# Adding a zero row to the last, 64-row tile of a K dimension of 448, and zero columns to its transposes, with earlier staging of Q and K and later Pool constants

## The chip, the cores and the metric

The kernel runs on one NeuronCore of a Trainium2 chip. Its metric is the device time of one execution in microseconds (us), as the median of several executions. A profile is the hardware's own record of one execution; its span is a little shorter than the time (204.2 us against 205.9 us for the same execution of the kernel before).

Engines are named as the profile names them: PE is TensorE (matmuls), PEld its weight loads, DVE is VectorE, ACT is ScalarE, POOL is GpSimd, SP issues most of the DMAs.

"Clock" is the share of PE's full clock that the chip granted. This kernel has windows of 3.41 us in which PE gets half of it.

## The reference

One transformer block on x of 2048 tokens by 448 (bf16): LayerNorm with conditioning, dilated local attention (16 heads of 28, window 8, step 2), LayerNorm again, an MLP of 448 to 1792 to 448, and two gated residuals.

```python
mod = (_silu(c) @ w_mod).reshape(c.shape[0], 6, 1, -1)
sa, ca, ga, sb, cb, gb = ...                      # six rows of 448
h = _layernorm(x) * (1 + ca) + sa
x = x + ga * _A_ref(h, A_wqkv, A_wo)              # qkv = h @ wqkv; attention; @ wo
h = _layernorm(x) * (1 + cb) + sb
x = x + gb * _B_ref(h, B_w1, B_b1, B_w2, B_b2)    # layernorm, gelu(y @ w1 + b1) @ w2 + b2
```

What matters is that D = 448 = 3 * 128 + 64. Every product that sums over D takes three tiles of 128 rows and one of 64.

## The kernel before

All work is added to a small planner as tasks with an engine, an assumed duration, and reads and writes. The planner runs a list schedule with these durations and emits the instructions in that order.

```python
S, D, H, DH, F = 2048, 448, 16, 28, 1792
KT, KR = 4, 64
KW = (128, 128, 128, KR)          # rows of each K tile
...
    # QK projection, for 2 or 4 token blocks (n = 256 or 512 columns), 8 groups
    for kt in range(KT):
        nc.tensor.matmul(pq.t[:], lhsT=wqk_m(kt, m), rhs=hT[0:KW[kt], kt, c0:c0 + n],
                         start=(kt == 0), stop=(kt == KT - 1))
...
    # V projection, once for each of 17 attention blocks
    for kt in range(KT):
        nc.tensor.matmul(pv.t[:], lhsT=hT[0:KW[kt], kt, k0:k0 + BK], rhs=Wv[0:KW[kt], kt, :],
                         start=(kt == 0), stop=(kt == KT - 1))
...
    # transposes of LN1's output; kt = 3 is 64 columns wide
    nc.tensor.transpose(out=ptr.t[0:KW[kt], k, bi * 128:(bi + 1) * 128],
                        in_=zbufs[b % NZ][:, kt * 128:kt * 128 + KW[kt]], identity=ident[:])
...
    # MLP: here the last tile has 65 rows already, since row 64 carries the bias
    kp = KW[kt] + (kt == KT - 1)
    nc.tensor.matmul(p1.t[:, f, :], lhsT=w1_s[0:kp, kt, (fq + f) * 128:(fq + f + 1) * 128],
                     rhs=yT.t[0:kp, kt, :], start=(kt == 0), stop=(kt == KT - 1))
```

The weights of Q and K are staged side by side in one tile and spread by head into `Wqk` (heads of 28 padded to 32); Q's spread is on DVE, most of K's on ACT. The conditioning columns (`ps_col`) are 32 matmuls of one column each, 8 of them with 64 rows. Attention itself uses small tiles on purpose: 28-row logits (`lt`) and 32-column sums (`pd`, `po`), four side by side in the array.

The softmax here doesn't subtract the row's maximum and nothing guards it: scores larger than these inputs give would overflow.

Of the kernel before, what the change touches and what calls it, by code (L numbers as in the profile page):

```python
# [9 lines left out]
BF16 = mybir.dt.bfloat16  # L10
ACT = mybir.ActivationFunctionType
# [3 lines left out]
DP = 512  # L15
KT, KR = 4, 64
KW = (128, 128, 128, KR)
HP = 32
FT = F // 128
WIN = 8  # L20
# [7 lines left out]
EPS = 1e-5  # L28
DEN_SCALE = 2.0 ** -32
EXP_SET = "natural_log_exp_and_others"  # L30
QKE = "ADAADAAD"
SPREAD = (("DVE", "DVE"), ("ACT", "DVE"))
PHASES = [
    (range(0, 5), [0]),
    (range(5, 9), [1, 2]),
# [164 lines left out]
def kernel(  # L200
# [35 lines left out]
    def sb(room, shape, dtype, name):  # L236
        return Buf(room, lambda: wk.tile(shape, dtype, name=name, tag=room, bufs=ROOM[room]), name)
# [36 lines left out]
    rs_all = cst.tile([128, 3, NBLK], FP32, name="rs_all")  # L274
    NX1P = 8
    NZ, NY, NV = 4, 4, 3
    zbufs = [cst.tile([128, D], BF16, name=f"zbuf{i}") for i in range(NZ)]
    ybufs = [cst.tile([128, DP], BF16, name=f"ybuf{i}") for i in range(NY)]
    vbufs = [cst.tile([128, H, HP], BF16, name=f"vbuf{i}") for i in range(NV)]
    x1p_ring = cst.tile([128, NX1P, D], FP32, name="x1p_ring")  # L280
    wm_st = sb("hm", [128, KT, 2 * D + KR], BF16, "wm_st")
    wqk_st = sb("hm", [128, KT, 2 * D + HP - DH], BF16, "wqk_st")
    wmod2 = [sb("hm", [128, KT, 2 * D], BF16, f"wmod2{i}") for i in range(2)]

    def tok_col(b):
# [27 lines left out]
    def load_x(b0, b1):  # L313
        load(lambda: nc.sync.dma_start(out=x_all[:, b0:b1, :], in_=xv[b0 // 8, :, b0 % 8:(b1 - 1) % 8 + 1, :]),
             (b1 - b0) * 128 * D * 2, [f"x{b}" for b in range(b0, b1)])
# [2 lines left out]
    add("DVE", 0.1, lambda: nc.vector.memset(one1[:], 1.0), writes=["one1"], rank_add=500)  # L318
    add("DVE", 0.1, lambda: nc.vector.memset(c_row[:, D:DP], 0.0), writes=["c_tail"], rank_add=500)
    add("ACT", 0.4, lambda: nc.scalar.dma_start(out=c_row[:, 0:D], in_=c), writes=["c_row"], late=2.0, rank_add=500)  # L320
    tbl0 = add("ACT", 1.28, lambda: nc.scalar.preload_act_table_set(EXP_SET), rank_add=400)
    load_x(0, 2)
    load_k(lambda: wm_st.t[:], w_mod[:, 0:2 * D + KR], "wm", [wm_st])
    load_k(lambda: wqk_st.t[:, :, 0:D + HP - DH], A_wqkv[:, 0:D + HP - DH], "wq", [wqk_st])
    load_k(lambda: wqk_st.t[:, :, D + HP - DH:], A_wqkv[:, D + HP - DH:2 * D + HP - DH], "wk", [wqk_st])
    load_x(2, 4)
    load_k(lambda: Wv[:], A_wqkv[:, 2 * D:3 * D], "wv")
    load_x(4, 8)
    for i in range(2):
        load_k(lambda i=i: wmod2[i].t[:], w_mod[:, (2 + 2 * i) * D:(4 + 2 * i) * D], f"wmod2{i}", [wmod2[i]])  # L330
    add("DVE", 0.3, lambda: nc.vector.memset(wo_s[:], 0.0), writes=["wo"], rank_add=400)
    wo_v = A_wo.rearrange("(ft r d) n -> r d ft n", r=4, d=DH)
    for r in range(4):
# [12 lines left out]
                F * D, [f"w2l{i}"])  # L346


    def pool(us, fn, writes, reads=(), rank_add=300):
        add("POOL", us, fn, writes=writes, reads=reads, rank_add=rank_add)  # L350

    pool(0.1, lambda: nc.gpsimd.memset(eps_col[:], EPS), ["eps"])
    pool(0.2, lambda: nc.gpsimd.memset(ident[:], 0.0), ["ident"])
    pool(0.3, lambda: nc.gpsimd.affine_select(out=ident[:], in_=ident[:], pattern=[[-1, 128]],
                                              compare_op=ALU.not_equal, fill=1.0, base=0, channel_multiplier=1),
         ["ident"])
    def one_row():
        nc.gpsimd.memset(one_cb[:], 0.0)
        nc.gpsimd.memset(one_cb[2 * HP:3 * HP, :], 1.0)
# [88 lines left out]
    def mod_cols():  # L448
        for v in range(2):
            for j in range(KT):  # L450
                for kt in range(KT):
                    nc.tensor.matmul(pscol.t[:, v * KT + j:v * KT + j + 1],  # L452
                                     lhsT=wm_st.t[0:KW[kt], kt, v * D + j * 128:v * D + (j + 1) * 128],
                                     rhs=silu_bf[0:KW[kt], kt:kt + 1], start=(kt == 0), stop=(kt == KT - 1))

    P.wrote(add("PE", 2.0, mod_cols, reads=["silu", "wma", "wmb"], bufs=[pscol, wm_st]), pscol)
    add("DVE", 0.08, lambda: nc.vector.tensor_copy(out=mod_col[:, 0:KT], in_=pscol.t[:, 0:KT]), bufs=[pscol],
        writes=["sa"])
    add("DVE", 0.08, lambda: nc.vector.tensor_scalar_add(out=mod_col[:, KT:2 * KT], in0=pscol.t[:, KT:2 * KT], scalar1=1.0),
# [18 lines left out]
    def front_ln(bs, on_act):  # L478
        for b in bs:
            stats(lambda b=b: x_all[:, b, :], [f"x{b}"], b, mv1, b)  # L480
        if on_act:
            rstd_act(mv1, 0, bs[0], len(bs))
        else:
            rstd_pool(mv1, 0, bs[0], len(bs))
        for b in bs:
            normalize(lambda b=b: zbufs[b % NZ][:], lambda b=b: x_all[:, b, :], mv1, 0, b, [f"x{b}"], [f"z{b % NZ}"])
        n = len(bs)
        c0 = tok_col(bs[0])
        for half, eng in enumerate(("DVE", "ACT")):
            ptr = ps_one([128, 2, 128 * n], "ptr", BF16)  # L490

            def tr(half=half, ptr=ptr):
                for bi, b in enumerate(bs):
                    for k in range(2):
                        kt = 2 * half + k
                        nc.tensor.transpose(out=ptr.t[0:KW[kt], k, bi * 128:(bi + 1) * 128],  # L496
                                            in_=zbufs[b % NZ][:, kt * 128:kt * 128 + KW[kt]],
                                            identity=ident[:])

            P.wrote(add("PE", 0.13 * n, tr, reads=["ident"] + [f"z{b % NZ}" for b in bs], bufs=[ptr]), ptr)  # L500
            for k in range(2):
                evac_h(2 * half + k, ptr, k, c0, 128 * n, eng, bs)

    def spread(half, k0, k1, eng):

        kw = KW[k0]
        key = "wq" if half == 0 else "wk"
        o = Wqk[0:kw, k0:k1, half]

        def i():  # L510
            a = wqk_st.t[0:kw, k0:k1, half * D:(half + 1) * D]
            return bass.AP(a.tensor, a.offset, [a.ap[0], a.ap[1], [DH, H], [1, HP]])

        reads = [h + ("a" if k0 < KT - 1 else "b") for h in ("wq", "wk")[0:half + 1]]
        if eng == "DVE":
            add("DVE", 0.08 + 0.134 * (k1 - k0), lambda: nc.vector.tensor_copy(out=o, in_=i()), reads=reads, bufs=[wqk_st], writes=[f"W{half}{k0}"])
        else:
            add("ACT", 0.17 + 0.366 * (k1 - k0), lambda: nc.scalar.copy(out=o, in_=i()), reads=reads, bufs=[wqk_st], writes=[f"W{half}{k0}"])

    def wqk_m(kt, m):  # L520
        return Wqk[0:KW[kt], kt, m // 4, m % 4 * 4:m % 4 * 4 + 4, :].rearrange("p r e -> p (r e)")

    def front_qk(bs, engs):
        n, c0 = 128 * len(bs), tok_col(bs[0])
        for m in range(8):
            pq = ps_one([128, n], "pq")

            def mm(m=m, pq=pq):
                for kt in range(KT):
                    nc.tensor.matmul(pq.t[:], lhsT=wqk_m(kt, m), rhs=hT[0:KW[kt], kt, c0:c0 + n],  # L530
                                     start=(kt == 0), stop=(kt == KT - 1))

            P.wrote(add("PE", 4 * n / 2400 + 0.02, mm,
                        reads=[f"W{m // 4}0", f"W{m // 4}{KT - 1}"]
                        + [f"h{kt}_{b}" for kt in range(KT) for b in bs], bufs=[pq]), pq)
            dst = (qT if m < 4 else kT)[:, m % 4, c0:c0 + n]
            w = [f"{'q' if m < 4 else 'k'}{m % 4}_{b}" for b in bs]
            if engs[m] == "D":
                add("DVE", 0.07 + n / 960, lambda dst=dst, pq=pq: nc.vector.tensor_copy(out=dst, in_=pq.t[:]), bufs=[pq],
                    writes=w)  # L540
            else:
                add("ACT", 0.13 + n / 1400, lambda dst=dst, pq=pq: nc.scalar.copy(out=dst, in_=pq.t[:]), bufs=[pq], writes=w)  # L542


    def mods():
        pb = ps_one([128, D], "pb")

        def mm():
            for kt in range(KT):
                for i in range(4):  # L550
                    nc.tensor.matmul(pb.t[HP * i:HP * i + HP], lhsT=silu_bc[0:KW[kt], kt, :],
                                     rhs=wmod2[i // 2].t[0:KW[kt], kt, i % 2 * D:(i % 2 + 1) * D],
                                     start=(kt == 0), stop=(kt == KT - 1), tile_position=(0, HP * i))

        P.wrote(add("PE", 1.1, mm, rank_add=150, reads=["silu_bc"] + [f"wmod2{i}{h}" for i in range(2) for h in "ab"],
                    bufs=[pb] + wmod2), pb)
        add("ACT", 0.6, lambda: nc.scalar.activation(out=mod_rows[:], in_=pb.t[:], func=ACT.Identity, bias=one_cb[:]),
            bufs=[pb], reads=["one_cb"], writes=["mod_rows"])
# [23 lines left out]
    def attention(b, tbl, prev_w1):  # L582
# [5 lines left out]

        def vmm():
            for kt in range(KT):  # L590
                nc.tensor.matmul(pv.t[:], lhsT=hT[0:KW[kt], kt, k0:k0 + BK], rhs=Wv[0:KW[kt], kt, :],  # L591
                                 start=(kt == 0), stop=(kt == KT - 1))

        P.wrote(add("PE", 0.76, vmm, reads=["wva", "wvb"] + PADK + [f"h{kt}_{t}" for kt in range(KT) for t in tb], bufs=[pv, vbuf]), pv)
        P.wrote(add("ACT", 0.45, lambda: nc.scalar.copy(out=vbuf.t[:, :, 0:DH],  # L595
                                                        in_=pv.t[:].rearrange("p (h d) -> p h d", h=H)),
                    bufs=[pv, vbuf], reads=["vpad"]), vbuf)
# [237 lines left out]
```

## Time and profile before

| kernel before | |
|---|---|
| time, median of 3 | 205.52 us (205.34 to 206.44) |
| profiled span, mean clock | 204.2 us, 0.982 |
| PE / DVE / ACT busy | 95% / 65% / 58% |
| half-clock windows in the profile | at 9.1 and 36.4 us, and one at the very end |

The page of the kernel before: busy time, then busy tenths in 40 slices of 5.1 us each, then the granted clock in tenths.

```profile
PE 193.9 (95%) x1709; PEld 107.3 (53%) x1709; DVE 132.5 (65%) x342; ACT 117.7 (58%) x168; POOL 45.1 (22%) x88
...
PE   7699997899999999999999999999999989999992
...
DVE  5476478989999859689813699585179668502102
...
PEclk9879999699999999999999999999999999999999
```

Its chain that ended last, by engine:

```profile
PE 85%; DMA 6%; DVE 5%; ACT 2%; SPq 0%; issue 0%; DVEq 0%
```

So PE limits. But how a busy PE spends its time doesn't show in busy shares. It shows on the row of the weight loads. Groups of lines, shapes kept apart; columns are busy us, mean ns, then idle time just before these instructions and what ended it:

```profile
L720 PEld LDWEIGHTS <-w_s 65*128 65x128 bf16 x112 | 10.8, 96 | 1.4
...
L530 PEld LDWEIGHTS <-Wqk 128*128 128x128 bf16 x120 | 9.3, 98 | 10.0 <-issue 4.2
...
L530 PEld LDWEIGHTS <-Wqk 64*128 64x128 bf16 x40 | 3.7, 93 | 14.2 <-issue 14.2
...
L591 PEld LDWEIGHTS <-hT 64*128 64x128 bf16 x17 | 1.6, 93 | 6.3 <-issue 6.3
```

The 40 weight loads of 64 rows at L530 (QK) have 14.2 us of idle before them for which the profile names no releaser ("issue"). The 112 loads of 65 rows at L720 (W1) have none. The timeline of the weight loads shows it beat by beat (start, duration, instruction, idle before):

```profile
20.46 0.44 PEld L530 LDWEIGHTS <-Wqk 64*128 64x128 bf16 x4 [0.21 <-issue]
21.11 0.44 PEld L530 LDWEIGHTS <-Wqk 64*128 64x128 bf16 x4 [0.21 <-issue]
21.75 0.44 PEld L530 LDWEIGHTS <-Wqk 64*128 64x128 bf16 x4 [0.21 <-issue]
```

Each group of four begins 0.65 us after the last, where four matmuls of 256 columns at their own pitch (110 ns) need 0.44 us. The missing 0.21 us stands before the 64-row load.

The windows view shows the stretch where other engines are full too (columns: window, length, then busy us and instructions of PE, PEld, DVE, ACT and POOL, granted clock, DMA share, GB/s):

```profile
24.00:30.00 6.00, 6.00 (x70) 2.49 (x69) 3.02 (x6) 5.18 (x9) 0.00 (x0) 1.00 0.27 65
30.00:36.00 6.00, 4.23 (x87) 2.39 (x88) 5.35 (x11) 6.00 (x10) 0.00 (x0) 1.00 0.95 301
36.00:42.00 6.00, 5.48 (x35) 1.71 (x34) 5.30 (x16) 3.49 (x7) 1.02 (x1) 0.72 0.87 269
42.00:48.00 6.00, 6.00 (x25) 1.92 (x24) 5.78 (x16) 2.04 (x4) 2.55 (x3) 1.00 0.01 3
```

### The profile page before, as it was taken

The page shows a single profiled execution, that of the slowest core. Times are in us where ns is not written, and L with a number is a line of the kernel's source. Part 1 is how long each engine was busy: PE and PEld are TensorE (multiplying, and loading weights), DVE is VectorE, ACT ScalarE, POOL GpSimd, SP SyncE. Part 2 cuts the span into 40 slices and gives each one's busy share as a digit, 9 for nine tenths or more (in the row PEclk, how much of TensorE's full clock was granted, in tenths as well). Part 3 has the DMA queues.
Part 4 walks back from the last instruction along what each step waited for, and adds up shares of the span by engine and source line. Part 5 has one row for each costly group of instructions (what it writes and reads, how often), then busy time and mean ns, then how long its engine had stood idle before and what let it go on. Part 6 is the DMA issues. An engine that isn't in the chain of part 4 may idle for free.

```text
span 204.2 us, 4212 instructions
## 1 busy us (share of the span) xinstructions
PE 193.9 (95%) x1709; PEld 107.3 (53%) x1709; DVE 132.5 (65%) x342; ACT 117.7 (58%) x168; POOL 45.1 (22%) x88
## 2 busy tenths in 40 slices
PE   7699997899999999999999999999999989999992
PEld 2445443233457346635584437468644747666750
DVE  5476478989999859689813699585179668502102
ACT  2246399626937997466568983674858175431230
POOL 8200200119242203134300053162032306200000
PEclk9879999699999999999999999999999999999999
DMA  6999239900110200010140100401200211201011
GB/s 189 299 333 259 83 93 328 315 10 3 27 29 0 53 3 0 5 26 0 26 55 0 48 0 0 100 0 29 67 3 16 60 41 34 42 9 48 3 44 45
DMA packets 19000, 13.91 MB, mean 68 GB/s; under 512 B 9246, under 2 KB 18403, under 8 KB 18980
## 3 DMA queue, kind: packets, MB, share of 16 engines
q1 hardware_dynamic: 18978, 13.64, 24.9%
q8 instruction: 13, 0.21, 0.5%
q14 instruction: 7, 0.06, 0.1%
q10 hardware_dynamic: 2, 0.00, 0.0%
HBM read 9.70 MB, written 1.84 MB: 56 GB/s over the span
## 4 chain that ended last, share of the span: by engine, by line
PE 85%; DMA 6%; DVE 5%; ACT 2%; SPq 0%; issue 0%; DVEq 0%
PE p L720 24%; PE p L740 21%; PE pq L530 17%; PE pw L670 6%; PE pv L591 6%; PE ptr L496 3%; DMA wm_st<-in_w_mod_dram 3%; DMA mod_bc<-mod_hbm 2%; PE lt L604 2%; PE pd L631 2%; PE po L635 1%; PE pwm L395 1%; DVE et L622 1%; PE ps_col L452 1%; DVE x_all L747 1%; DVE oT L650 1%
## 5 line engine op out<-in xcount | busy, mean ns | idle before, releaser
L720 PE MATMUL p<-yT,w_s 128*128 128x256 bf16 x448 | 52.3, 272 | 0.2 <-ACT hm L727 0.2
L727 ACT ACTIVATE hm<-p 128x1024 bf16<-128x1024 f32 (+1 forms) x32 | 28.4, 916 | 34.2 <-PE p L720 34.1
L720 PEld LDWEIGHTS <-w_s 128*128 128x128 bf16 x448 | 43.3, 97 | 9.0 <-issue 1.1
L740 PE MATMUL p<-w_s,hm 128*128 128x448 bf16 x224 | 47.6, 353 | 0.0
L530 PE MATMUL pq<-hT,Wqk 128*128 128x512 bf16 (+3 forms) x160 | 38.3, 350 | 0.4 <-DVE oT L650 0.4
L420 POOL TENSOR_TENSOR rs_all<-tv_all,neg_half 128x1 f32<-128x1 f32 (+1 forms) x35 | 21.6, 624 | 69.1 <-DVE tv_all L417 69.0
L614 ACT ACTIVATE et<-lt 128x976 bf16<-128x976 f32 x34 | 31.8, 990 | 3.1 <-PE lt L604 3.1
L622 DVE TENSOR_TENSOR et<-et,mask 128x976 bf16<-128x976 bf16 x34 | 22.6, 664 | 16.6 <-ACT et L614 16.5
L700 POOL TENSOR_TENSOR x1p_ring<-x_all,gbb_bc 128x448 f32<-128x448 bf16 x16 | 17.2, 1074 | 60.6 <-DVE x_all L674 42.9
L747 DVE TENSOR_TENSOR x_all<-p,x1p_ring 128x448 bf16<-128x448 f32 x16 | 9.9, 621 | 31.1 <-PE p L740 31.0
L740 PEld LDWEIGHTS <-hm 128*128 128x128 bf16 x224 | 20.6, 98 | 17.8 <-issue 0.8
L530 PEld LDWEIGHTS <-Wqk 128*128 128x128 bf16 (+1 forms) x160 | 13.0, 97 | 24.3 <-issue 18.5
L641 ACT ACTIVATE lden<-pd 128x488 f32<-128x488 f32 x17 | 9.9, 580 | 18.5 <-PE pd L631 18.5
L402 DVE BATCH_NORM_STATS2 st_all<-x_all 128x6 f32<-128x448 bf16 x32 | 19.1, 617 | 1.4 <-DMA x_all<-in_A_x_dram 1.3
L591 PE MATMUL pv<-Wv,hT 128*128 128x448 bf16 x68 | 17.2, 357 | 0.0
L670 PE MATMUL pw<-wo_s,oT 128*128 128x448 bf16 x64 | 14.6, 353 | 1.6 <-DVE oT L650 0.5
L542 ACT CAST qT<-pq 128x512 bf16<-128x512 f32 (+1 forms) x15 | 7.4, 505 | 10.2 <-PE pq L530 10.1
L650 DVE SCALAR_TENSOR_TENSOR oT<-po,rden 128x484 bf16<-128x484 f32 x17 | 11.1, 655 | 1.4 <-ACT rden L643 1.4
L674 DVE TENSOR_TENSOR x_all<-pw,x_all 128x448 bf16<-128x448 f32 x16 | 10.0, 622 | 2.8 <-PE pw L670 2.7
L591 PEld LDWEIGHTS <-hT 128*128 128x128 bf16 x68 | 5.4, 97 | 10.4 <-issue 7.5
L643 ACT ACTIVATE rden<-lden 128x488 f32<-128x488 f32 x17 | 10.6, 621 | 0.4
L595 ACT CAST vbuf<-pv 128x448 bf16<-128x448 f32 x17 | 8.8, 551 | 2.3 <-PE pv L591 2.3
(77 smaller groups left out, 177.3 us busy)
## 6 DMA issues: line engine op xcount, KB each, us to landing
out_dram<-x_all SPq DMA_DIRECT2D x8, 224.0 KB, 2.0
w_s<-in_B_w_dram SPq DMA_DIRECT2D x2, 784.0 KB, 11.5
wmod<-in_w_mod_dram SPq DMA_DIRECT2D x2, 672.0 KB, 7.4
w_s<-in_B_w_dram SPq DMA_DIRECT2D x1, 1344.0 KB, 9.3
x_all<-in_A_x_dram SPq DMA_DIRECT2D x1, 896.0 KB, 8.5
wm_st<-in_w_mod_dram SPq DMA_DIRECT2D x1, 720.0 KB
x_all<-in_A_x_dram SPq DMA_DIRECT2D x2, 224.0 KB
x_all<-in_A_x_dram SPq DMA_DIRECT2D x1, 448.0 KB
```

What stands on the lines that cost most here:

```text
L402: add("DVE", 0.53, lambda: nc.vector.bn_stats(out=st_all[:, sl, :], in_=src()), reads=key, writes=[f"st{sl}"])
L420: lambda: nc.gpsimd.tensor_tensor(out=rs_all[:, which, b0:b0 + n], in0=tv_all[:, which, b0:b0 + n], in1=neg_half[:, 0:n], op=ALU.pow),
L530: nc.tensor.matmul(pq.t[:], lhsT=wqk_m(kt, m), rhs=hT[0:KW[kt], kt, c0:c0 + n], start=(kt == 0), stop=(kt == KT - 1))
L591: nc.tensor.matmul(pv.t[:], lhsT=hT[0:KW[kt], kt, k0:k0 + BK], rhs=Wv[0:KW[kt], kt, :], start=(kt == 0), stop=(kt == KT - 1))
L614: ex = add("ACT", 0.87, lambda half=half: nc.scalar.activation(out=et.t[:, 2 * half:2 * half + 2], in_=lts[half].t[:, :, 0:4 * EQ].rearran ...
L622: nc.vector.tensor_tensor(out=ev, in0=ev, in1=mask[:], op=ALU.mult)
L650: nc.vector.scalar_tensor_tensor(out=oT[:, :, o0:o0 + BQ], in0=po.t[:], scalar=DEN_SCALE, in1=rden.t[:, :, 0:BQ], op0=ALU.mult, op1=ALU.mult)
L670: nc.tensor.matmul(pw.t[:], lhsT=oT[:, ft, c0:c0 + 128], rhs=wo_s[:, ft, :], start=(ft == 0), stop=(ft == 3))
L700: nc.gpsimd.tensor_tensor(out=x1p_ring[:, t % NX1P, :], in0=x_all[:, t, :], in1=gbb2_bc[:], op=ALU.add)
L720: nc.tensor.matmul(p1.t[:, f, :], lhsT=w1_s[0:kp, kt, (fq + f) * 128:(fq + f + 1) * 128], rhs=yT.t[0:kp, kt, :], start=(kt == 0), stop=(kt ...
L727: gl = add("ACT", 0.18 + nf * 0.183, lambda fq=fq, nf=nf, p1=p1: nc.scalar.activation(out=hm.t[:, fq:fq + nf, :], in_=p1.t[:, 0:nf, :], fu ...
L740: nc.tensor.matmul(p2.t[:], lhsT=hm.t[:, ft, bi * 128:(bi + 1) * 128], rhs=w2_s[:, ft, :], start=(ft == 0), stop=(ft == FT - 1))
```

## The change

The intent: give every last K tile 65 rows, of which row 64 is zero on both sides, and transpose full 128 columns, of which the last 64 are zero. No result changes. The zero rows need one-time memsets. With these come three moves: Q and K are staged in two separate blocks, so that Q's spread needn't wait for K's DMA; K's spread goes from ACT to DVE; and Pool's constants wait until a memset in a buffer that comes free after the conditioning.

```diff
+KE = (128, 128, 128, KR + 1)
-SPREAD = (("DVE", "DVE"), ("ACT", "DVE"))
+SPREAD = (("DVE", "DVE"), ("DVE", "DVE"))
-    zbufs = [cst.tile([128, D], BF16, ...)]
+    zbufs = [cst.tile([128, DP], BF16, ...)]                     # DP = 512
-    wqk_st = sb("hm", [128, KT, 2 * D + HP - DH], BF16, "wqk_st")
+    wqk_st = sb("hm", [128, 2, KT, D + HP - DH], BF16, "wqk_st")
+    # DVE memsets of row 64 of the last tile: wqk_st (2), wm_st, hT, Wv; of columns D:DP of zbufs (4)
+    # POOL memsets of row 64 of wmod2 (2); the second is the "gate"
-        add("POOL", us, fn, writes=writes, reads=reads, rank_add=rank_add)
+        add("POOL", us, fn, ..., order_after=[gate] if gated else [])   # all but eps and ident
-                     lhsT=wm_st.t[0:KW[kt], ...], rhs=silu_bf[0:KW[kt], kt:kt + 1], ...
+                     lhsT=wm_st.t[0:KE[kt], ...], rhs=silu_bf[0:KE[kt], kt:kt + 1], ...
-    P.wrote(add("PE", 2.0, mod_cols, ...
+    P.wrote(add("PE", 1.2, mod_cols, ...
-    nc.tensor.transpose(out=ptr.t[0:KW[kt], k, ...], in_=zbufs[b % NZ][:, kt * 128:kt * 128 + KW[kt]], ...)
+    nc.tensor.transpose(out=ptr.t[:, k, ...], in_=zbufs[b % NZ][:, kt * 128:(kt + 1) * 128], ...)
     # ... and KW -> KE in the matmuls of QK, V and the modulation rows, and in the spread
```

More of the change, by code (lines that the diff above doesn't have):

```diff
@@ L276 @@
     NZ, NY, NV = 4, 4, 3
-    zbufs = [cst.tile([128, D], BF16, name=f"zbuf{i}") for i in range(NZ)]
+    zbufs = [cst.tile([128, DP], BF16, name=f"zbuf{i}") for i in range(NZ)]
     ybufs = [cst.tile([128, DP], BF16, name=f"ybuf{i}") for i in range(NY)]
@@ L320, with zero @@
     add("ACT", 0.4, lambda: nc.scalar.dma_start(out=c_row[:, 0:D], in_=c), writes=["c_row"], late=2.0, rank_add=500)
+    z_row = slice(KR, KR + 1)
+    def zero(us, what, keys, bufs=(), eng="DVE", rank=450, order_after=()):
+        e = nc.vector if eng == "DVE" else nc.gpsimd
+        return add(eng, us, lambda: e.memset(what(), 0.0), writes=keys, bufs=bufs, rank_add=rank, order_after=order_after)
     tbl0 = add("ACT", 1.28, lambda: nc.scalar.preload_act_table_set(EXP_SET), rank_add=400)
+    for i in range(2):
+        zero(0.15, lambda i=i: wqk_st.t[z_row, i, KT - 1, :], [f"wqk0{i}"], [wqk_st], rank=460)
+    zero(0.3, lambda: wm_st.t[z_row, KT - 1, :], ["wm0"], [wm_st])
+    zero(0.6, lambda: hT[z_row, KT - 1, :], ["hT0"])
+    zero(0.15, lambda: Wv[z_row, KT - 1, :], ["Wv0"])
+    for i in range(NZ):
+        zero(0.08, lambda i=i: zbufs[i][:, D:DP], ["ztail"])
     load_x(0, 2)
     load_k(lambda: wm_st.t[:], w_mod[:, 0:2 * D + KR], "wm", [wm_st])
-    load_k(lambda: wqk_st.t[:, :, 0:D + HP - DH], A_wqkv[:, 0:D + HP - DH], "wq", [wqk_st])
-    load_k(lambda: wqk_st.t[:, :, D + HP - DH:], A_wqkv[:, D + HP - DH:2 * D + HP - DH], "wk", [wqk_st])
+    load_k(lambda: wqk_st.t[:, 0], A_wqkv[:, 0:D + HP - DH], "wq", [wqk_st])
+    load_k(lambda: wqk_st.t[:, 1], A_wqkv[:, D:2 * D + HP - DH], "wk", [wqk_st])
     load_x(2, 4)
@@ L330 @@
         load_k(lambda i=i: wmod2[i].t[:], w_mod[:, (2 + 2 * i) * D:(4 + 2 * i) * D], f"wmod2{i}", [wmod2[i]])
+    gate = None
+    for i in range(2):
+        gate = zero(0.8, lambda i=i: wmod2[i].t[z_row, KT - 1, :], [f"wmod0{i}"], [wmod2[i]], "POOL", 600 - 200 * i, [gate] if gate else [])
     add("DVE", 0.3, lambda: nc.vector.memset(wo_s[:], 0.0), writes=["wo"], rank_add=400)
@@ L346, in load_mlp, with pool @@
                 F * D, [f"w2l{i}"])
-    def pool(us, fn, writes, reads=(), rank_add=300):
-        add("POOL", us, fn, writes=writes, reads=reads, rank_add=rank_add)
-    pool(0.1, lambda: nc.gpsimd.memset(eps_col[:], EPS), ["eps"])
-    pool(0.2, lambda: nc.gpsimd.memset(ident[:], 0.0), ["ident"])
+    def pool(us, fn, writes, reads=(), rank_add=300, gated=True):
+        add("POOL", us, fn, writes=writes, reads=reads, rank_add=rank_add, order_after=[gate] if gated else [])
+    pool(0.1, lambda: nc.gpsimd.memset(eps_col[:], EPS), ["eps"], gated=False, rank_add=900)
+    pool(0.2, lambda: nc.gpsimd.memset(ident[:], 0.0), ["ident"], gated=False, rank_add=800)
     pool(0.3, lambda: nc.gpsimd.affine_select(out=ident[:], in_=ident[:], pattern=[[-1, 128]],
                                               compare_op=ALU.not_equal, fill=1.0, base=0, channel_multiplier=1),
-         ["ident"])
+         ["ident"], gated=False, rank_add=800)
     def one_row():
@@ L452, in mod_cols @@
                     nc.tensor.matmul(pscol.t[:, v * KT + j:v * KT + j + 1],
-                                     lhsT=wm_st.t[0:KW[kt], kt, v * D + j * 128:v * D + (j + 1) * 128],
-                                     rhs=silu_bf[0:KW[kt], kt:kt + 1], start=(kt == 0), stop=(kt == KT - 1))
-    P.wrote(add("PE", 2.0, mod_cols, reads=["silu", "wma", "wmb"], bufs=[pscol, wm_st]), pscol)
+                                     lhsT=wm_st.t[0:KE[kt], kt, v * D + j * 128:v * D + (j + 1) * 128],
+                                     rhs=silu_bf[0:KE[kt], kt:kt + 1], start=(kt == 0), stop=(kt == KT - 1))
+    P.wrote(add("PE", 1.2, mod_cols, reads=["silu", "wma", "wmb", "wm0"], bufs=[pscol, wm_st]), pscol)
     add("DVE", 0.08, lambda: nc.vector.tensor_copy(out=mod_col[:, 0:KT], in_=pscol.t[:, 0:KT]), bufs=[pscol],
@@ L485, in front_ln @@
         for b in bs:
-            normalize(lambda b=b: zbufs[b % NZ][:], lambda b=b: x_all[:, b, :], mv1, 0, b, [f"x{b}"], [f"z{b % NZ}"])
+            normalize(lambda b=b: zbufs[b % NZ][:, 0:D], lambda b=b: x_all[:, b, :], mv1, 0, b, [f"x{b}"], [f"z{b % NZ}"])
         n = len(bs)
@@ L495, in tr @@
                         kt = 2 * half + k
-                        nc.tensor.transpose(out=ptr.t[0:KW[kt], k, bi * 128:(bi + 1) * 128],
-                                            in_=zbufs[b % NZ][:, kt * 128:kt * 128 + KW[kt]],
-                                            identity=ident[:])
-            P.wrote(add("PE", 0.13 * n, tr, reads=["ident"] + [f"z{b % NZ}" for b in bs], bufs=[ptr]), ptr)
+                        nc.tensor.transpose(out=ptr.t[:, k, bi * 128:(bi + 1) * 128],
+                                            in_=zbufs[b % NZ][:, kt * 128:(kt + 1) * 128], identity=ident[:])
+            P.wrote(add("PE", 0.13 * n, tr, reads=["ident", "ztail"] + [f"z{b % NZ}" for b in bs], bufs=[ptr]), ptr)
             for k in range(2):
@@ L504, in spread @@
     def spread(half, k0, k1, eng):
-        kw = KW[k0]
+        kw = KE[k0]
         key = "wq" if half == 0 else "wk"
@@ L510, in i @@
         def i():
-            a = wqk_st.t[0:kw, k0:k1, half * D:(half + 1) * D]
+            a = wqk_st.t[0:kw, half, k0:k1, :]
             return bass.AP(a.tensor, a.offset, [a.ap[0], a.ap[1], [DH, H], [1, HP]])
-        reads = [h + ("a" if k0 < KT - 1 else "b") for h in ("wq", "wk")[0:half + 1]]
+        reads = [("wq", "wk")[half] + ("a" if k0 < KT - 1 else "b"), f"wqk0{half}"]
         if eng == "DVE":
@@ L520, in wqk_m @@
     def wqk_m(kt, m):
-        return Wqk[0:KW[kt], kt, m // 4, m % 4 * 4:m % 4 * 4 + 4, :].rearrange("p r e -> p (r e)")
+        return Wqk[0:KE[kt], kt, m // 4, m % 4 * 4:m % 4 * 4 + 4, :].rearrange("p r e -> p (r e)")
     def front_qk(bs, engs):
@@ L529, in mm @@
                 for kt in range(KT):
-                    nc.tensor.matmul(pq.t[:], lhsT=wqk_m(kt, m), rhs=hT[0:KW[kt], kt, c0:c0 + n],
+                    nc.tensor.matmul(pq.t[:], lhsT=wqk_m(kt, m), rhs=hT[0:KE[kt], kt, c0:c0 + n],
                                      start=(kt == 0), stop=(kt == KT - 1))
             P.wrote(add("PE", 4 * n / 2400 + 0.02, mm,
-                        reads=[f"W{m // 4}0", f"W{m // 4}{KT - 1}"]
+                        reads=[f"W{m // 4}0", f"W{m // 4}{KT - 1}", "hT0"]
                         + [f"h{kt}_{b}" for kt in range(KT) for b in bs], bufs=[pq]), pq)
@@ L550, in mm @@
                 for i in range(4):
-                    nc.tensor.matmul(pb.t[HP * i:HP * i + HP], lhsT=silu_bc[0:KW[kt], kt, :],
-                                     rhs=wmod2[i // 2].t[0:KW[kt], kt, i % 2 * D:(i % 2 + 1) * D],
+                    nc.tensor.matmul(pb.t[HP * i:HP * i + HP], lhsT=silu_bc[0:KE[kt], kt, :],
+                                     rhs=wmod2[i // 2].t[0:KE[kt], kt, i % 2 * D:(i % 2 + 1) * D],
                                      start=(kt == 0), stop=(kt == KT - 1), tile_position=(0, HP * i))
-        P.wrote(add("PE", 1.1, mm, rank_add=150, reads=["silu_bc"] + [f"wmod2{i}{h}" for i in range(2) for h in "ab"],
+        P.wrote(add("PE", 1.1, mm, rank_add=150, reads=["silu_bc"] + [f"wmod2{i}{h}" for i in range(2) for h in "ab"] + ["wmod00", "wmod01"],
                     bufs=[pb] + wmod2), pb)
@@ L590, in vmm @@
             for kt in range(KT):
-                nc.tensor.matmul(pv.t[:], lhsT=hT[0:KW[kt], kt, k0:k0 + BK], rhs=Wv[0:KW[kt], kt, :],
+                nc.tensor.matmul(pv.t[:], lhsT=hT[0:KE[kt], kt, k0:k0 + BK], rhs=Wv[0:KE[kt], kt, :],
                                  start=(kt == 0), stop=(kt == KT - 1))
-        P.wrote(add("PE", 0.76, vmm, reads=["wva", "wvb"] + PADK + [f"h{kt}_{t}" for kt in range(KT) for t in tb], bufs=[pv, vbuf]), pv)
+        P.wrote(add("PE", 0.76, vmm, reads=["wva", "wvb", "Wv0", "hT0"] + PADK + [f"h{kt}_{t}" for kt in range(KT) for t in tb], bufs=[pv, vbuf]), pv)
         P.wrote(add("ACT", 0.45, lambda: nc.scalar.copy(out=vbuf.t[:, :, 0:DH],
```

## The prediction

> **What bounds the kernel now.** TensorE: the page gives PE 95% busy, and the chain that ended last is 85% PE. The wait view shows about 7 us of idle PE in 204. But "busy" hides a cost inside the QKV groups. Start to start, a 128-row matmul after a 128-row one takes 216 ns (512 columns), 189 (448), 110 (256). Into a 64-row matmul it is 312, 285 and 205 ns, out of it 319, 293 and 212: about 0.1 us each way. The W1 groups, whose last tile has 65 rows, show none of it (108 in, 113 out). The groups of lines show the same as "issue" idle of the weight loads at the QK line: 18.5 us in 57 gaps. The Trainium skill, "TensorEngine Tiling (Array Packing)", Key Properties, says that changing the tiling mode drains TensorE; this trace agrees, with about 0.1 us for each change.
>
> **What the change removes** (counts times measured surplus):
> - 24 QK groups of 512 columns and 16 of 256, 0.2 us each, less those followed by another small mode anyway: 7.3 us.
> - 17 V groups: 3.0 us.
> - 16 transposes 64 columns wide: 160 in, 176 out against 56 ns: 3.6 us.
> - conditioning, 8 times (96 + 107 against 32 + 32 ns): 1.0 us; modulation rows 0.2.
> Sum: about 15 us of PE. Attention's own mode changes (28-row logits, 32-column sums) stay.
>
> **What it adds and moves.** About ten one-time memsets on DVE, 2.2 us by estimate from the 0.81 us memset of 896 words; DVE idled 1.3 us there, so LN1 starts about 1 us later, mostly hidden behind the conditioning weights (landing 7.35 us). The K spread leaves ACT (1.47 us) for DVE (0.69). The Q spread no longer waits for K's DMA (9.7 us; its own packets were in at 7.9). Pool's constants go from 0.8-6.4 to about 9-16 us; they no longer stall a small DVE operation (0.87 us at 4.6) but may stall a spread.
>
> **How much is critical.** QK began at 13.3 us, after fillers from 10.7; I expect 10.5 to 11.5, worth about 2.3 us with conditioning and the first transposes. Thereafter PE saves about 13 us. From 60 us on (5 us of it) I expect all to count. Between 14 and 60 (8 us) part is lost: ACT is full at 24-36, DVE 5.3-6.0 of 6 us at 30-66, and the chain at 25-36 goes through the modulation rows' DMA (1.6 + 4.5 us) with PE idle, followed by a half-clock window (36.4-39.9, about 1.9 us). I count 60% there.
>
> **Prediction:** 205.5 - 2.3 - 5 - 4.7 = 193.5 us, range 189.5 to 198.5. Faster by over 2%: 0.95; within 2%: 0.04; slower: 0.01.
>
> **What would show it.** QK groups at 0.86 us (512) and 0.43 (256) rather than 1.07 and 0.64, V groups 0.76 rather than 0.97; "issue" idle of weight loads at the QK line nearly gone; first QK at 10.5-11.5 us; modulation rows at 18-20 rather than 25; PE share lower (about 93%), more waits on DVE and ACT at 20-60 us; the last MLP tiles (from 175) unchanged in length.
>
> **What would make it wrong.** If 65 rows did not count as a full tile here, nearly nothing would come. If DVE and ACT limit all of 14-60 us, or idle PE brings another half-clock window, I get 198. If the earlier modulation lets the whole first phase slide, up to 16 us come. Pool's late constants colliding with DVE's spreads could cost 1 us at the front.

## The result, and the profile after

| | before | after |
|---|---|---|
| time, median (fast runs, 4 each) | 205.43 us | 197.05 us (195.17 to 198.07) |
| ratio of fast runs | | 0.957 (0.949 to 0.965) |
| the same again beside the experiments, 5 rounds | 205.67 us | 195.1 us, ratio 0.948 (0.944 to 0.952) |
| profiled span, mean clock | 204.2 us, 0.982 | 193.5 us, 0.991 |

A ratio is the mean time of one kernel's fast runs over that of the other's in the same rounds, so not quite the ratio of the medians. A run more than 1.5% above the fastest of its kernel is called slow and left out of ratios, though not of medians.

The page after, the same lines, and its chain by engine:

```profile
PE 180.2 (93%) x1707; PEld 110.5 (57%) x1707; DVE 134.9 (70%) x352; ACT 114.4 (59%) x167; POOL 48.2 (25%) x90
...
PE   7799967994999999999999999999999989999991
...
DVE  6998999999899778984758942980588677211102
...
PEclk9999999999799999999999999999999999999999
...
PE 73%; DVE 11%; ACT 8%; DMA 3%; issue 2%; SPq 0%; DVEq 0%
```

PE fell from 85 to 73% of the chain, while DVE and ACT together rose from 7 to 19%. The weight loads after, by shape:

```profile
L546 PEld LDWEIGHTS <-Wqk 128*128 128x128 bf16 x120 | 11.9, 103 | 10.5 <-issue 1.9 <-DVE w_s L591 0.2
...
L546 PEld LDWEIGHTS <-Wqk 65*128 65x128 bf16 x40 | 4.1, 102 | 3.4 <-issue 0.3
...
L607 PEld LDWEIGHTS <-hT 65*128 65x128 bf16 x17 | 1.7, 97 | 1.6
```

The idle named "issue" before the last K tile's load went from 14.2 to 0.3 us (QK) and from 6.3 us to none (V). In the timeline, where before four loads ended in a gap, sixteen now run in one piece, 1.83 us for four groups:

```profile
17.94 1.83 PEld L546 LDWEIGHTS <-Wqk 128*128 128x128 bf16 x16
```

The start-to-start times, worked out from the start times of the trace's matmuls (medians in ns), say the same:

| from → to | before (64 rows) | after (65 rows) |
|---|---|---|
| QK 512 columns: full → full | 216 | 216 |
| full → last tile / last tile → full | 312 / 319 | 215 / 219 |
| QK 256: full → last / last → full | 205 / 212 | 108 / 114 |
| V 448: full → last / last → full | 285 / 293 | 189 / 193 |
| transposes: full → 64-wide / 64-wide → full | 160 / 176 | 56 (all full) |

From the same start times each profile can be split over PE's whole timeline. "Stream" is each matmul's own pitch (416.7 ns per 1000 columns plus 2 ns for a full tile, which fits the 216, 189 and 110 ns above; the side-by-side small tiles count once for four). "Mode changes" is the surplus of pairs whose tile sizes differ (rows or columns in the classes up to 32, up to 64, up to 128), taken from undisturbed pairs of the same kind. What is left is waiting, or half clock where it falls in such a window. The changes are counted on the weight loads, of which no record is missing. Fillers and small surpluses are 9.1 and 9.0 us, the two ends of the span 5.6 us.

| us | before | after |
|---|---|---|
| stream | 151.8 | 151.4 |
| mode changes | 21.9 (220 of them) | 6.2 (63) |
| waiting | 13.3 | 19.8 |
| half clock | 2.7 | 1.5 |
| span | 204.2 | 193.5 |

So 15.7 us of changes went, and 6.5 us came back as waiting. Half clock took 1.2 us less than before in these two profiles, so waiting and half clock together rose by 5.3 us. The waits view of PE after shows where (its longest entries; before, none after 14 us was over 1.0 us in total):

```profile
PE pd L647 <- DVE et L638: 1.5, 1, 1.5
...
PE pw L686 <- DVE hT L487: 1.1, 1, 1.1
PE pv L607 <- DVE oT L666: 1.1, 1, 1.1
PE lt L620 <- ACT et L630: 1.0, 2, 0.6
...
PE ptr L513 <- ACT vbuf L611: 0.8, 1, 0.8
```

All of these but one of the two `lt` waits lie between 26 and 48 us, where DVE has no room at all:

```profile
24.00:30.00 6.00, 4.20 (x94) 2.63 (x92) 6.00 (x16) 5.74 (x10) 1.36 (x1) 1.00 0.58 212
30.00:36.00 6.00, 4.91 (x42) 2.40 (x42) 6.00 (x14) 2.90 (x5) 0.00 (x0) 1.00 1.06 310
36.00:42.00 6.00, 6.00 (x62) 2.77 (x60) 6.00 (x14) 3.75 (x7) 3.53 (x4) 1.00 0.33 115
42.00:48.00 6.00, 3.57 (x34) 1.90 (x36) 6.00 (x21) 4.67 (x9) 2.61 (x3) 0.96 0.04 8
```

DVE is busy 6.00 of 6 us in all four windows (3.02 to 5.78 before), while PE is down to 3.57 us in the last. That lull is followed by a half-clock window at 47.5 to 50.9 us. DVE's timeline there shows what PE's `pd` was waiting for (start, duration, instruction):

```profile
39.02 1.10 DVE L442 TENSOR_SCALAR z<-x_all,mv,rs_all 128x448 bf16<-128x448 bf16 x1
...
40.35 1.23 DVE L701 TENSOR_TENSOR h<-z,mod_bc 128x448 bf16<-128x448 bf16 x1
...
44.24 0.59 DVE L591 TENSOR_TENSOR w_s<-w_s,mod_bc 128x896 bf16<-128x896 bf16 x1
44.75 0.66 DVE L638 TENSOR_TENSOR et<-et,mask 128x976 bf16<-128x976 bf16 x1
45.33 1.42 DVE L442 TENSOR_SCALAR ybuf<-h,mv,rs_all 128x448 bf16<-128x448 bf16 x2
46.67 0.65 DVE L638 TENSOR_TENSOR et<-et,mask 128x976 bf16<-128x976 bf16 x1
```

The second mask multiplication (46.67) stands behind the normalisation for LN2 (45.33, 1.42 us), and PE waits for it. The first `z` and `h` shown took 1.10 and 1.23 us; their neighbours of the same shape took 0.38.

The chain that ended last shows whose pace this stretch follows (start, duration, what). Before, it runs through PE from 40.76 to 59.2 us, but for 1.45 us of ACT:

```profile
40.76 0.91 PE pw L670 x4
41.67 2.04 PE pq L530 x8
43.71 0.86 PE pw L670 x4
44.57 4.19 PE pq L530 x16
```

After, it runs through DVE from 29.64 to 47.9 us, with less than 0.2 us of anything else:

```profile
29.64 1.15 DVE wo_s L582 x2
31.61 1.23 DVE et L638 x2
...
45.33 1.42 DVE ybuf L442 x2
...
48.55 1.61 PE pw L686 x4
```

So in this execution, with this order of work, PE waited for DVE there. In a second profile of the same kernel (the repeat, below) the chain lies on DVE from 34.7 to 47.3 us.

### The profile page after: what moved, and what is told of

Its sections match the earlier page's. It is cut to its first block, busy times and chain, and to the rows that moved or that the text cites. A ratio compares the mean times of both kernels' runs of the same rounds, so it can differ in the third digit from the quotient of the medians.

```text
span 193.5 us, 4233 instructions
## 1 busy us (share of the span) xinstructions
PE 180.2 (93%) x1707; PEld 110.5 (57%) x1707; DVE 134.9 (70%) x352; ACT 114.4 (59%) x167; POOL 48.2 (25%) x90
## 4 chain that ended last, share of the span: by engine, by line
PE 73%; DVE 11%; ACT 8%; DMA 3%; issue 2%; SPq 0%; DVEq 0%
PE p L736 25%; PE p L756 22%; PE pq L546 9%; PE pw L686 6%; PE pv L607 4%; ACT et L630 3%; DMA wm_st<-in_w_mod_dram 3%; DVE et L638 2%; PE lt L620 2%; PE pd L647 1%; PE po L651 1%; PE pwm L412 1%; ACT lden L657 1%; DVE oT L666 1%; DVE x_all L763 1%
## 5 line engine op out<-in xcount | busy, mean ns | idle before, releaser
L437 POOL TENSOR_TENSOR rs_all<-tv_all,neg_half 128x1 f32<-128x1 f32 (+1 forms) x35 | 21.7, 629 | 52.8 <-DVE tv_all L434 52.7
L546 PE MATMUL pq<-hT,Wqk 128*128 128x512 bf16 (+3 forms) x160 | 31.9, 350 | 0.2 <-ACT mod_rows L573 0.2
L716 POOL TENSOR_TENSOR x1p_ring<-x_all,gbb_bc 128x448 f32<-128x448 bf16 x16 | 17.7, 1110 | 57.3 <-DVE x_all L690 37.3
L638 DVE TENSOR_TENSOR et<-et,mask 128x976 bf16<-128x976 bf16 x34 | 22.0, 654 | 6.0 <-ACT et L630 6.0
L546 PEld LDWEIGHTS <-Wqk 128*128 128x128 bf16 (+1 forms) x160 | 16.0, 103 | 13.9 <-issue 2.2
L686 PE MATMUL pw<-wo_s,oT 128*128 128x448 bf16 x64 | 15.2, 367 | 1.9 <-DVE hT L487 1.1
L607 PE MATMUL pv<-Wv,hT 128*128 128x448 bf16 x68 | 15.2, 353 | 1.1 <-DVE oT L666 1.1
L686 PEld LDWEIGHTS <-oT 128*128 128x128 bf16 x64 | 6.0, 100 | 8.1 <-DVE oT L666 1.4
## 6 DMA issues: line engine op xcount, KB each, us to landing
w_s<-in_B_w_dram SPq DMA_DIRECT2D x2, 784.0 KB, 10.8
```

The source lines that it names most:

```text
L437: lambda: nc.gpsimd.tensor_tensor(out=rs_all[:, which, b0:b0 + n], in0=tv_all[:, which, b0:b0 + n], in1=neg_half[:, 0:n], op=ALU.pow),
L546: nc.tensor.matmul(pq.t[:], lhsT=wqk_m(kt, m), rhs=hT[0:KE[kt], kt, c0:c0 + n], start=(kt == 0), stop=(kt == KT - 1))
L607: nc.tensor.matmul(pv.t[:], lhsT=hT[0:KE[kt], kt, k0:k0 + BK], rhs=Wv[0:KE[kt], kt, :], start=(kt == 0), stop=(kt == KT - 1))
L638: nc.vector.tensor_tensor(out=ev, in0=ev, in1=mask[:], op=ALU.mult)
L686: nc.tensor.matmul(pw.t[:], lhsT=oT[:, ft, c0:c0 + 128], rhs=wo_s[:, ft, :], start=(ft == 0), stop=(ft == 3))
L716: nc.gpsimd.tensor_tensor(out=x1p_ring[:, t % NX1P, :], in0=x_all[:, t, :], in1=gbb2_bc[:], op=ALU.add)
```

## The experiments

My theory had two parts. First, a change between a 128-row and a 64-row tile costs PE about 0.1 us each way, and the gain comes from taking 157 such changes away. Second, what came back did so because DVE bounds the stretch from the first QK matmul to the first W1. Rivals: a 64-row matmul is slow in itself; the moves carry much of the gain; ACT, DMA latency or the granted clock took the rest back.

Twelve kernels ran, five rounds each beside the kernel before. The first four ran on one chip, the other eight on a second; the median of the kernel before was 205.61 to 205.67 us in each set, so ratios are compared across sets.

### The changed kernel again

> The changed kernel again, beside the others on one chip. If the chip and the half-clock windows behave as before: about 0.957 of the kernel before (196 to 198 us where that takes 205.4), first QK matmul at about 11 us. The profile shows whether the idle PE at 26-32 and 43-48 us and a half-clock window after it come again or were chance.

195.1 us, ratio 0.948. The waits came again at 25-31 and 43-48 us. The half-clock windows came at 7.8 and 28.3 us this time, in place of 47.5. Over the ten runs of this kernel, the seven with a granted clock of 0.974 or more took 194.4 to 196.9 us, and the three at 0.965 took 197.2 to 198.1. Two of the four runs behind the first median of 197.05 us were of the latter kind, and a third was at 0.974. The work is the same in all ten, so most of the difference between 197.05 and 195.1 us goes with the clock. It is a correlation: above 0.974 the order doesn't hold (195.2 and 195.8 us at 0.991, 194.4 to 195.2 at 0.981), and whether a lull of PE brings the window or the other way round can't be told from the times alone.

### The rows alone, and the moves alone

Rows alone: the changed kernel with staging, the spread's engines and Pool's constants as before.

```diff
-SPREAD = (("DVE", "DVE"), ("DVE", "DVE"))
+SPREAD = (("DVE", "DVE"), ("ACT", "DVE"))
-    wqk_st = sb("hm", [128, 2, KT, D + HP - DH], ...)
+    wqk_st = sb("hm", [128, KT, 2 * D + HP - DH], ...)     # one block again, loads and reads as before
-    ... order_after=[gate] if gated else [])
+    ... order_after=[])                                    # Pool as before
```

> The 65-row last tiles and the full-width transposes alone; staging of Q and K, engines of the spread and Pool constants as before. Theory (mode changes carry the gain): 197 to 200 us, at least three quarters of the gain of the whole change; QK groups at 0.86 and 0.43 us, first QK at about 12.5 to 13 us. Rival (the moves carry half or more): 201 us or more.

Moves alone: the changed kernel, 64-row tiles again.

```diff
-KE = (128, 128, 128, KR + 1)
+KE = (128, 128, 128, KR)
-    nc.tensor.transpose(out=ptr.t[:, k, ...], in_=zbufs[b % NZ][:, kt * 128:(kt + 1) * 128], ...)
+    nc.tensor.transpose(out=ptr.t[0:KW[kt], k, ...], in_=zbufs[b % NZ][:, kt * 128:kt * 128 + KW[kt]], ...)
```

> The moves alone (split staging, K spread on DVE, later Pool constants, the memsets), with 64-row tiles and 64-wide transposes again. Theory: only the front moves, first QK at 11 to 12 us, 203 to 204.5 us, with QK groups still 1.07 and 0.64 us. Rival (the moves carry half or more of the gain): 201 us or less.

| | ratio (95%) | first QK | mode changes | waiting + half clock |
|---|---|---|---|---|
| before | 1 | 13.33 us | 220, 21.9 us | 16.0 us |
| moves alone | 0.998 (0.994 to 1.002) | 13.46 us | 214, 21.3 us | 16.8 us |
| rows alone | 0.946 (0.940 to 0.952) | 11.99 us | 68, 6.7 us | 21.7 us |
| whole change, the repeat | 0.948 (0.944 to 0.952) | 10.91 us | 63, 6.2 us | 20.5 us |

The rows carry the whole gain; the moves carry nothing that these intervals (0.4 to 0.6% each way) would show, alone or on top. My expectation for the moves missed: I thought Q's earlier spread would bring the first QK to 11 to 12 us. It stayed at 13.5, because the conditioning matmuls and the transposes, still with mode changes, came first (transposes at 9.57 us, against 7.72 us in the whole change); in that profile a half-clock window from 8.65 to 15.5 us also lay over them. On top of the rows, the moves do bring the first QK 1.1 us forward, but no time comes of it.

### The transposes back

```diff
-    nc.tensor.transpose(out=ptr.t[:, k, ...], in_=zbufs[b % NZ][:, kt * 128:(kt + 1) * 128], ...)
+    nc.tensor.transpose(out=ptr.t[0:KW[kt], k, ...], in_=zbufs[b % NZ][:, kt * 128:kt * 128 + KW[kt]], ...)
```

> The whole change but for the transposes, whose last one is 64 columns wide again: 16 transposes at 0.22 us each are 3.6 us of PE, nearly all before 80 us. If PE time there counted fully: 3.6 us slower than the change. Since I hold that DVE and ACT limit part of that stretch: 1 to 2.5 us slower. If a narrow transpose costs nothing: no difference.

Ratio 0.954 (0.949 to 0.959), against 0.948: 1.2 us slower, for 3.5 us more of mode changes (94 of them, 9.7 us). The two intervals overlap, but the fast runs hardly do: 195.6 to 196.7 us here, 194.4 to 195.8 for the changed kernel. This is the cleanest view of where savings go, since PE, DVE and ACT run their instructions in the same order in both kernels. From the first QK to the first W1:

| us | mode changes | waiting + half clock | length |
|---|---|---|---|
| transposes back | 3.8 | 9.9 | 40.6 |
| whole change | 1.7 | 11.5 | 40.2 |
| whole change, the repeat | 1.7 | 10.8 | 39.6 |

2.1 us of drains less, 0.9 to 1.6 us of waiting and half clock more; the stretch is only 0.4 to 1.0 us shorter. About half or more of what PE gains there it waits away. From the first W1 on, the drains differ by 0.9 us and the length by 0.8: there it arrives.

### Two small tiles next to each other

The kernel before, with the 64-row tile first in every second QK group. The same matmuls, rows and bytes.

```diff
-    for kt in range(KT):
+    for i, kt in enumerate((0, 1, 2, 3) if m % 2 == 0 else (3, 0, 1, 2)):
         nc.tensor.matmul(pq.t[:], lhsT=wqk_m(kt, m), rhs=hT[0:KW[kt], kt, c0:c0 + n],
-                         start=(kt == 0), stop=(kt == KT - 1))
+                         start=(i == 0), stop=(i == KT - 1))
```

> The kernel before, but in every second QK group the 64-row tile comes first, so that in back-to-back groups two 64-row tiles stand next to each other; same matmuls, same rows, same bytes. Theory A (a change of mode costs about 0.1 us each way): half of the QK surplus goes, a pair of 512-column groups takes about 1.93 instead of 2.14 us, 64-row after 64-row 216 ns (512) and 110 ns (256); about 3.5 us less PE, 202 to 203.5 us. Rival B (a 64-row matmul or its weight load is slow by itself): 64-row after 64-row keeps the surplus, pairs 2.1 us, 205.4 us.

Ratio 0.990 (0.985 to 0.995), 203.59 us. A 64-row matmul after a 64-row one starts 226 ns later at 512 columns and 119 ns at 256 (4 of each), against 318 and 212 ns when a full one follows, and 216 and 110 ns full to full. The 10 ns over full to full are not the row count's either: they stand on the second start after a change of mode, whatever the tile. In the kernel before, a full tile after a full one takes 227 ns at 512 columns and 120 at 256 right after a change, and 216 and 109 to 110 later in the group. So the row count costs nothing that shows, and a change of mode some 95 to 104 ns and then about 10 more. Rival B falls. The weight loads agree (14.2 us of "issue" before):

```profile
L530 PEld LDWEIGHTS <-Wqk 64*128 64x128 bf16 x40 | 3.1, 93 | 10.2 <-issue 10.0
```

The size missed: I expected 3.5 us less PE, and it was 1.3 us of changes (203 in place of 220). Only in 8 of 20 pairs did the two small tiles stand back to back; the planner puts other work between the rest. The profiled run had no half-clock window before its end (clock 0.998), which helped it beyond that.

### Less DVE work

Both kernels without the seven multiplications of w2 by the gate. Their outputs are wrong, which doesn't matter for the times.

```diff
-            add("DVE", 0.55, lambda i=i: nc.vector.tensor_tensor(
-                out=w2_s[:, 2 * i:2 * i + 2, :], in0=..., in1=gb_bc..., op=ALU.mult), ...)
+            P.writer[f"w2_{i}"] = P.writer["w2l0" or "w2l1"]     # W2 waits for the load alone
```

> The changed kernel without the 7 multiplications of w2 by the gate (4.3 us of DVE between 44 and 58 us); wrong result on purpose. Theory (after the change DVE is what the stretch 25-60 us waits for, which took back part of the gain): 2 to 4 us faster than the changed kernel. Rival (PE still limits, or what was lost is the granted clock): within 1 us of the changed kernel.

> The same taken from the kernel before; wrong result on purpose. Theory: there PE was the limit, so 4.3 us less DVE work gives 1 us or less, clearly less than in the changed kernel. If it gives as much as there, DVE limited both and the change didn't turn the limit.

After: 0.949, against 0.948 with them. Before: 0.999. So 4.3 us less DVE work gave nothing in either. My expectation fell, and the timeline suggests why: six of the seven multiplications come after 48 us, once the long waits are over. The seventh (44.24 us) stood in DVE's chain. Without it the second mask came 1.4 us earlier (45.23 us), but the normalisation behind it took 1.21 us, PE waited 1.3 us for `oT` in place of the mask, and W1 still began at 51.34 us. The test took work from the wrong place; it does not speak against a limit of DVE before 44 us, but it shows that a full DVE row is no proof of one.

### More DVE work, more ACT work

LN1's statistics of blocks 4 to 15 taken twice, in both kernels:

```diff
+            if b >= 4:
+                add("DVE", 0.53, lambda b=b: nc.vector.bn_stats(out=st_all[:, b, :], in_=x_all[:, b, :]),
+                    reads=[f"x{b}"], writes=[f"st{b}"])
             stats(lambda b=b: x_all[:, b, :], [f"x{b}"], b, mv1, b)
```

> The changed kernel with the statistics of LN1 taken twice for tokens blocks 4 to 15, the second the same as the first: 12 more DVE operations, about 6.5 us at 0.54 us pitch, all between 12 and 50 us. Theory (after the change DVE bounds the stretch from the first QK to the first W1, which is why about 5 us of the saved PE time came back as waits): 4 to 6.5 us slower than the changed kernel, first W1 later by as much. Rival (that stretch is bound by ACT, by DMA latencies or still by PE): under 2 us.

> The same 12 operations added to the kernel before. Theory: PE was the limit there and DVE had room (3.0 to 5.9 us busy in 6), so clearly less than in the changed kernel: 1 to 3 us. Rival (DVE bounded that stretch before the change too, and the change turned nothing): the same slowdown as there.

And ACT's copies of QK for blocks 4 to 11 done twice, in the changed kernel:

```diff
+                for _ in range(2 if bs[0] in (4, 8) else 1):
                     add("ACT", 0.13 + n / 1400, lambda dst=dst, pq=pq: nc.scalar.copy(out=dst, in_=pq.t[:]), ...)
```

> The changed kernel with each QK copy of ACT done twice for the blocks 4 to 7 and 8 to 11: 10 more ACT operations of about 0.5 to 0.6 us, 5 to 6 us. Theory DVE: ACT is full only at 18-30 us, so 1 to 2.5 us slower, clearly less than with the same time added to DVE. Rival (ACT bounds the stretch): 4 us or more.

| | ratio (95%) | against its own base |
|---|---|---|
| changed, 6.5 us more DVE | 0.968 (0.964 to 0.973) | +4.2 us |
| before, 6.5 us more DVE | 1.015 (1.011 to 1.019) | +3.1 us |
| changed, 5 to 6 us more ACT | 0.933 (0.930 to 0.937) | -3.0 us |

(The differences are those of the ratios, times 205.6 us.) DVE time in this stretch is worth about two thirds of itself after the change, in line with the theory. But it was worth half of itself before, and with the noise the two costs (3.2 to 5.1 and 2.3 to 3.9 us by the intervals shown) overlap. The planner also reordered PE in both kernels (from 25.6 us on in the changed one, from 30.4 in the other), so these runs measure the work and a new order together. That the change turned the limit from PE to DVE is not shown by them; DVE work cost time in this stretch already before.

The third result I had not foreseen under any theory: more ACT work made the kernel faster. The added work can hardly have done that. What else changed is the order, which the planner chose anew for the longer ACT tasks: DVE's from 34 us on, PE's from 41. With it the lull at 43-48 us is gone. Its windows, to compare with the last two of the changed kernel above:

```profile
36.00:42.00 6.00, 5.48 (x31) 2.58 (x29) 6.00 (x22) 3.22 (x7) 3.69 (x5) 1.00 0.30 100
42.00:48.00 6.00, 5.32 (x68) 3.01 (x67) 6.00 (x15) 6.00 (x11) 2.69 (x4) 1.00 0.23 45
```

DVE is just as full, but PE is busy 5.32 us of 42-48 in place of 3.57. It takes QK and then W1 (from 47.8 us, not 51.3) ahead of the attention sums that waited for the second mask, which now come at 51.4 us. The chain that ended last leaves DVE at 41.0 us, in place of 47.9. No half-clock window follows, the profile's clock is 0.999, and the runs' times are 190.5 to 193.3 us, median 192.2. The clock is not the reason: at the same 0.991, four of these runs took 192.1 to 192.3 us, and two of the changed kernel 195.2 and 195.8. This kernel, useless copies and all, beats both; that the order is the cause, and would do as well without the copies, is likely but was not run.

### Pool not delayed

```diff
-    ... order_after=[gate] if gated else [])
+    ... order_after=[])
```

> The changed kernel with Pool's constants free to start at once again. Theory: the delay of Pool is worth under 1 us in all: the small DVE operations at 4.5-6 us get slower, silu about 0.5 us later, but the spreads at 9.5-11.8 us, which are 1.16 and 0.95 us against 0.69 and 0.27 beside Pool, get faster; within 1 us of the changed kernel. Rival (the gate is what brings the front forward): first QK 1 us later and the whole 1 us or more slower.

Ratio 0.949, against 0.948; first QK at 10.97 us. The delay of Pool is worth nothing measurable.

### Pool's residual sums later

In `out_proj` the task is removed; in `mlp` it comes back behind the first two W1 groups.

```diff
-        add("POOL", 1.05, x1p, reads=[f"x{t}", "gbb2"], writes=[f"x1p{t % NX1P}"])
+            if g < 2:
+                t = 2 * j + g
+                add("POOL", 1.05, ..., reads=[f"x{t}", "gbb2"], writes=[f"x1p{t % NX1P}"], order_after=[wm])
```

> The changed kernel with Pool's addition for the last residual (1.1 us each, two SBUF inputs) put behind the first W1 groups of its tile, in place of right after the output projection, where DVE operations with SBUF operands stand at 1.10 and 1.23 us beside it against 0.38 alone. Theory (these collisions are part of what DVE lacks in the stretch to the first W1): 0.5 to 1.5 us faster than the changed kernel. Rival (they cost nothing that counts, or only move): within 0.5 us.

Ratio 0.956 (0.953 to 0.958): 1.6 us slower than the changed kernel, not faster. The planner's order changed here too (first W1 at 49.3 us), so this doesn't tell what the collisions cost. It tells that moving these sums isn't a gain.

## Why the prediction was right or wrong

The class and the range held: 197.05 us, and 195.1 us in the repeat, against 193.5 us in a range of 189.5 to 198.5.

- **What is removed** was right in size and in cause. Predicted: about 15 us of PE, at 0.1 us a change. Measured: 157 changes and 15.7 us. The Trainium skill, "TensorEngine Tiling (Array Packing)", Key Properties, states the drain; the adjacent small tiles showed that the change of mode, not the row count, costs (226 ns against 318).
- **The front**: first QK expected at 10.5 to 11.5 us, measured 11.09. But the reason was partly wrong. I gave Q's earlier spread and the moves a share; the rows alone brought 13.33 to 11.99, the moves alone nothing, and the last 1.1 us of the two together did not reach the total.
- **From the first QK to the first W1** (13.3 to 59.1 us before, 11.1 to 51.3 after) the length fell by 5.5 us for 8.4 us of changes removed (10.1 to 1.7), while waiting and half clock rose from 6.9 to 11.5. That looks like the 60% I counted, but 1.6 us of it is matmul work that moved behind the first W1 (four QK and four output-projection matmuls). Without it, 3.9 of 8.4 us arrived, or 46%; the match of the number is partly luck.
- **From the first W1 on** I expected all of 5 us to count. 5.6 us of changes went, and the length fell by 3.0 us: 1.6 us is the work that moved there, and 1.1 us is more waiting. This term was mis-sized by 2 us. In sum the span fell by 10.7 us (2.2 + 5.5 + 3.0), where I had counted 12; the miss here and the moved work before it partly cancel.
- **The half clock** I named as a risk, with 198 us if idle PE brought another window. One came after the lull in the profiled run, which still took 195.17 us at a clock of 0.991; the runs at 0.965 took 197 to 198. So it goes with the first median, 197.05 us. Why the clock differs from run to run is not shown.
- **The signs**: groups of QK and V, "issue" idle, PE at 93%, more waits on DVE and ACT at 26-48 us, and the unchanged end (48.2 us from the last logits before, 48.0 after) came as written. The modulation rows did not: 22.2 us, where I had written 18 to 20. In the new order, PE's 16 matmuls for them come at 20.3 us and ACT then runs two exponentials first.

What stays open: how much of the 6.5 us of new waiting is DVE's ceiling and how much the planner's order. In the order that ran, the chain goes through DVE from 29.6 to 47.9 us, and equal order with fewer drains (the transposes) shows that PE no longer sets the pace there alone. More DVE work costs, but it cost before as well. A kernel with another order under the same full DVE is 3 us faster. So the order is probably a large part; a hard limit of DVE isn't shown.

## What to carry to other kernels

A last K tile of 64 rows is not a cheap tile: between full tiles, it costs PE two changes of mode, 0.2 us in all here, and one zero row on both sides (65 rows) takes that away for the price of some memsets (here about 2.5 us of DVE in all at the start, hidden: the first conditioning matmul came at 6.66 us, against 6.69 before). Look for it on the weight-load row, as "issue" idle before the small shape; the busy share of PE hides it. And when PE time is taken out of a kernel whose order comes from a planner, count the waits again afterwards: a full engine beside it and the order it works in decide how much arrives, and a PE lull can be followed by a half-clock window on top (PE was busy 1.08 of 3.41 us before the one at 47.5 us).

## What the Trainium skill lacked or had wrong

- "TensorEngine Tiling (Array Packing)", Key Properties, says that changing the tiling mode drains TensorE, but gives no cost. Here it is 95 to 104 ns each way at 256, 448 and 512 columns alike, and about 10 ns on the start after that.
- The same page doesn't say that an operand of 64 rows takes a small mode without a tile position being asked for, nor that 65 rows count as a full tile. Here 65 rows after 128 cost nothing (215 ns against 216 at 512 columns), and leaving them 3 to 5 ns.
- The same page, "When to Use Tiling", advises row tiling for a contract dimension up to 64. It says nothing of a lone 64-row remainder of a longer dimension. Between full tiles, that remainder is slower here than a full tile, by about 0.2 us a QK or V group.
- "TensorE: Matmul & The Clock Gate", Part 1, puts the half clock after at least one idle window of about 3.4 us. The windows here are 3.413 us long, as it says, but the ones before them were not idle: by the records PE was busy 1.08 of 3.41 us before the window at 47.5 us of the changed kernel, 1.74 before that at 36.4 us of the kernel before, and 1.62 before that at 28.3 us in the repeat. Counted in steps of 3.413 us from the recorded windows, over all 14 profiles, the 13 full-clock steps with at most 1.77 us of PE busy were all followed by half clock, and none with 2.31 us or more was, the kernels' ends left out; between, both occurred. In the repeat, 1.11 us busy of 3.41 from 43.43 us on brought no window: this lull lay across two steps, of 2.53 and 1.80 us.
